# Chunk attention and a bilinear feed-forward layer: DMA transposes issued from ScalarE's queue, loads of units 5 to 9 earlier in SyncE's

## The chip, the cores and the metric

The kernel runs on one core of a Trainium2 chip. The metric is the device time of an execution in microseconds. TensorE (PE) does the matmuls, VectorE (DVE), ScalarE (ACT) and GpSimd (POOL) work element by element, and SyncE (SP) only issues DMAs here. Each engine works through its own instructions in order.

## The reference

```python
batch, n_heads, seq, head_dim = (8, 8, 576, 64)
n_tokens, d_model, d_ff = (4608, 512, 1536)
...
q_c, k_c, v_c = ...                      # (B, H, 9 chunks, 64, 64)
scores = scale * np.matmul(q_c, k_c.transpose(0, 1, 2, 4, 3))
scores = scores - np.max(scores, axis=-1, keepdims=True)
attn = np.exp(scores)
attn = attn / (np.sum(attn, axis=-1, keepdims=True) + 1e-09)
out = np.matmul(attn, v_c)
...
x = attn_out.transpose(0, 2, 1, 3).reshape(B * S, H * D)
a = x @ w_a
b = x @ w_b
return (a * b @ w_out).astype(np.float32)
```

Attention stays within chunks of 64 tokens. Its result, 4608 tokens of 512 values, goes through a layer with two hidden products a and b of 1536 values, multiplied element by element, and an output product back to 512 values. Inputs and result are float32.

## The kernel before

**Tiling.** Tokens are worked in 9 blocks K of 512, and each block in two units of 256 tokens, so that there are 18 units u. A unit is four chunks of 64 tokens with all eight heads. Unit u belongs to block u // 2. Matmuls are in bf16 and accumulate in PSUM.

**A unit's way to its attention.** `load_unit(u)` brings q, k and v of the unit from HBM into three float32 tiles `f32[u % 3][x]`, each in two DMAs of 256 KB (line 123), or in four of 128 KB where the unit crosses from one batch entry to another. `cast_unit(u)` casts them to bf16 on GpSimd (line 171): q and k into `qkb[u % 2]`, v into `vb[u % 3]`. `turn_unit(u)` is one DMA transpose of 512 KB from `qkb[u % 2]` to `qkT[u % 3]` (line 215). Then come, on TensorE, `scores(u)` (line 233, into the PSUM tile PS), on ScalarE `expo(u)` (line 244), and later `sums(u)` (line 250) and `values(u)` (line 266); ScalarE takes a logarithm and an exponential for the reciprocal (lines 276, 280), and `normalise` on VectorE (line 285) writes x transposed, `xT`. Units 0 to 3 are turned on TensorE with helpers of their own; the DMA transpose serves units 4 to 17.

**The layer.** `ffn(K, ft)` is one of 12 steps of a block: four matmuls for b and four for a (line 397), each 128x128 by 128x512, into two of the four PSUM banks of the ring F. `ffn_close` copies b to SBUF on ScalarE (line 408, tile `bsb`), and VectorE multiplies it with a into `ab[ft]` (line 409). In block 1 the first seven steps are done in two halves of 256 tokens. The output product is `outs` in blocks 0 and 1 (lines 419 and 429), and `outs_fast` from block 2 on (lines 466 to 511), which needs fewer products but sums of the weights, `sum_wo(i)` on GpSimd (lines 453 to 456), and of a·b, `sum_ab`. In `outs_fast` ScalarE copies m3 and m4 (lines 495 and 501).

**The order.** It is written out by hand (`tc.manual_schedule`), and the instructions of each engine stand in the order of the program. `slot(uv, us)` puts attention between steps: sums and values of unit uv, then scores of unit us; the exponent and the normalisation that follow wait in the list `late`, and `step()` emits one of them before each step. In the steady part, blocks 2 to 8, `slot` comes after steps 1 and 8, `cast_unit(u + 1)` one step later, `turn_unit(u + 1)` and `load_unit(u + 3)` three steps later. Every load, store and transpose is issued from SyncE, one behind the other. The transitional part is blocks 0 and 1, where the weights have just been loaded and units 4 to 9 are brought in; its order is listed step by step, and it is this part that the change rewrites.

**Synchronisation.** The framework that builds the program adds the waits. A DMA waits for its data and for its buffer; its completion is counted on one of eight counters, and a DMA also waits until the one before it on the same counter has landed.

Of the kernel before, what the change touches and what calls it, by code (L numbers as in the profile page):

```python
# [11 lines left out]
def kernel(  # L12
# [10 lines left out]
    nc = tc.nc  # L23
# [57 lines left out]
    NP = NFT // 2  # L81
# [25 lines left out]
    def nextF():  # L107
        return ring("f", F)
# [9 lines left out]
    def load_natural(u, x, src, eng):  # L118

        t = f32[u % NF32][x]  # L120
        for g in range(2):
            for p, n, b, s0 in runs(u, g):
                eng.dma_start(  # L123
                    out=t[p:p + n, g * 512:(g + 1) * 512].rearrange("p (h d) -> p h d", h=H),
                    in_=src[b, :, s0:s0 + n, :].transpose([1, 0, 2]),
                )
# [47 lines left out]
    def cast_qk(u, x, eng):  # L174
        copy(eng, qkb[u % 2][:, x, :], f32[u % NF32][x])

    def cast_pairs(u, x, eng):
        copy(
            eng,
            qkb[u % 2][:, x, :].rearrange("p (r h d) -> p h r d", r=2, h=H),  # L180
            f32[u % NF32][x].rearrange("p (h r d) -> p h r d", h=H, r=2),
        )

    def cast_v(u, eng, pieces=1):
        n = 1024 // pieces
        for i in range(pieces):
            copy(eng, vb[u % 3][:, n * i:n * i + n], f32[u % NF32][2][:, n * i:n * i + n])
# [26 lines left out]
    def transpose_dma(u, eng):  # L214
        eng.dma_start_transpose(
            out=qkT[u % 3], in_=qkb[u % 2].rearrange("p x c -> p (x c)")
        )

    def scores(u, pairs=False):
        t = qkT[u % 3]  # L220
        tp = t[:, 0:8, :].rearrange("p (r m) t -> p m r t", r=2)
        for g in range(2):
            for m in range(4):
                c = g * 256 + m * 64
                for j in range(2):
                    for cl in range(2):
                        o = PS[cl * 64:cl * 64 + 64, j, c:c + 64]
                        qt = t[j * 64:j * 64 + 64, 4 * g + m, cl * 64:cl * 64 + 64]
                        if pairs:
                            n = (2 * g + cl) * 32  # L230
                            o = o.rearrange("p (t r) -> p r t", r=2)
                            qt = tp[j * 64:j * 64 + 64, m, :, n:n + 32]
                        nc.tensor.matmul(  # L233
                            o,
                            t[j * 64:j * 64 + 64, 8 + 4 * g + m, cl * 64:cl * 64 + 64],
                            qt,
                            start=True,
                            stop=True,
                        )
# [6 lines left out]
    def sums(u, SU, c0=0, c1=512):  # L246
        e = E[u % 2]
        for j in range(2):
            for cl in range(2):
                nc.tensor.matmul(  # L250
                    SU[cl][j * 64:j * 64 + 64, c0:c1],
                    ones[cl * 64:cl * 64 + 64, :],
                    e[cl * 64:cl * 64 + 64, j, c0:c1],
                    start=True,
                    stop=True,
                )

    def values(u):
        e = E[u % 2]
        for g in range(2):  # L260
            for m in range(4):
                c = g * 256 + m * 64
                for cl in range(2):
                    for j in range(2):
                        h = 2 * m + j
                        nc.tensor.matmul(  # L266
                            PA[j * 64:j * 64 + 64, cl, c:c + 64],
                            vb[u % 3][cl * 64:cl * 64 + 64, g * 512 + h * 64:g * 512 + h * 64 + 64],
                            e[cl * 64:cl * 64 + 64, j, c:c + 64],
                            start=True,  # L270
                            stop=True,
                        )

    def log_sums(u, SU):
        for cl in range(2):
            nc.scalar.activation(out=lns[:, cl, :], in_=SU[cl], func=AF.Ln)  # L276

    def inverse(u, cl=None):
        s = slice(0, 2) if cl is None else slice(cl, cl + 1)
        nc.scalar.activation(out=inv[u % 2][:, s, :], in_=lns[:, s, :], func=AF.Exp, scale=-1.0)  # L280
# [132 lines left out]
    def ffn(K, ft, us=(0, 1)):  # L413
        banks = nextF(), nextF()
        ffn_products(K, ft, us, range(NKT), banks)
        ffn_close(K, ft, us, banks)
# [20 lines left out]
    def outs(K, tgs):  # L437
        o = [nextF() for _ in tgs]
        for ft in range(NFT):
            for k, tg in enumerate(tgs):  # L440
                out_products(tg, ft, o[k])
        for k, tg in enumerate(tgs):
            out_close(K, tg, o[k])
# [5 lines left out]
    def sum_wo(i, eng):  # L449

        b = staged["o", i].rearrange("p (x c) -> p x c", x=4)
        y = wsum[:, i]
        eng.tensor_tensor(out=y[:, 0:2], in0=b[:, 0:4:2], in1=b[:, 1:4:2], op=ADD)  # L453
        eng.tensor_tensor(out=y[:, 2], in0=b[:, 1], in1=b[:, 3], op=SUB)  # L454
        eng.tensor_tensor(out=y[:, 3], in0=b[:, 2], in1=b[:, 0], op=SUB)  # L455
        eng.tensor_tensor(out=y[:, 4], in0=b[:, 0], in1=b[:, 3], op=ADD)
# [64 lines left out]
    with tc.manual_schedule():  # L521
# [10 lines left out]
        V, A, G = nc.vector, nc.scalar, nc.gpsimd  # L532
# [100 lines left out]
        def load_unit(u, xs=(0, 1, 2)):  # L633
            if u < NU:
                for x in xs:
                    load_natural(u, x, (q, k, v)[x], nc.sync)

        def cast_unit(u, xs=(0, 1, 2)):
            if u < NU:
                for x in xs:  # L640
                    if x < 2:
                        cast_qk(u, x, G)
                    else:
                        cast_v(u, G)

        def turn_unit(u):
            if u < NU:
                transpose_dma(u, nc.sync)

        def turn_pairs(u, x, engs):  # L650
            evacuate_pairs(u, x, transpose_pairs(u, x), engs)
# [3 lines left out]
        def drain():  # L655
            while late:
                fn, a = late.pop(0)
                fn(*a)

        def slot(uv, us, pairs=False, short=False):  # L660


            drain()
            if uv is not None:
                SU = nextF(), nextF()
                sums(uv, SU)
                values(uv)
                log_sums(uv, SU)
                if short:
                    for cl in range(2):  # L670
                        late.extend([(inverse, (uv, cl)), (normalise, (uv, cl))])
                else:
                    inverse(uv)
                    late.extend([(normalise, (uv, 0)), (normalise, (uv, 1))])
            if us is not None:
                scores(us, pairs)
                late.append((expo, (us,)))

        def step():
            if late:  # L680
                fn, a = late.pop(0)
                fn(*a)
# [26 lines left out]
        cast_pairs(3, 1, G)  # L709
        cast_unit(3, (2,))  # L710
        cast_pairs(2, 1, V)
        load_unit(5, (0,))
        o = nextF(), nextF()
        for ft in range(NFT):
            for tg in range(2):
# [23 lines left out]
        slot(None, 3, True)  # L739
        drain()  # L740
        cast_unit(4)
        turn_unit(4)
        load_unit(5, (1, 2))
        load_unit(6)
        cast_unit(5)

        for ft in range(7):
            step()
            ffn(1, ft, (0,))
            if ft == 1:  # L750
                slot(3, None, short=True)
            if ft == 3:
                turn_unit(5)
                load_unit(7)
        for ft in range(7):
            step()
            ffn(1, ft, (1,))
            if ft == 3:
                slot(None, 4)
                cast_unit(6)  # L760
        for ft in range(7, NFT):
            step()
            ffn(1, ft)
            if ft == 8:
                turn_unit(6)
                load_unit(8)
                sum_wo(1, G)
            if ft == 10:
                slot(4, 5)
                sum_wo(2, G)  # L770
                cast_unit(7)
        for tg in range(4):
            step()
            outs(1, (tg,))
            if tg == 1:
                slot(5, 6)
                turn_unit(7)
                load_unit(9)
                for i in range(3, NP):
                    sum_wo(i, G)  # L780
        for K in range(2, NBLK):
            for s in range(NFT + 2):
                step()
# [44 lines left out]
```

## Time and profile before

| | |
|---|---|
| time, median of 13 runs | 328.43 us (326.3 to 331.25) |
| the profiled execution: time, span | 328.94 us, 327.2 us |
| PE busy | 309.3 us (95%) |
| DVE, ACT, POOL busy | 185.8 (57%), 133.1 (41%), 124.9 (38%) us |
| DMA moved | 55.00 MB, mean 168 GB/s |
| DMA transposes (line 215) | 14, issued by SyncE, 5.0 us from issue to landing (median) |
| loads of 256 KB (line 123) | 28 each of q, k and v, 4.2 to 4.4 us to landing (median) |

The span is the time between the first and the last instruction that the profile shows; the profiled execution's own time is 1.7 us longer. A busy share is an average over the whole span: what a wait costs is to be read from the stage in which it stands. In the profile's timelines SPq is SyncE's queue of DMA issues; an issue's length is not the time until its data have landed. The text in square brackets at the end of a line is the idle time of the engine just before it, and what ended it.

### The profile page before, as it was taken

What the parts mean: (1) busy time and instruction counts of PE and PEld (TensorE: products, weight loads), DVE (VectorE), ACT (ScalarE), POOL (GpSimd) and SP (SyncE); (2) the same over time, 40 slices, a digit from 0 to 9 for tenths busy, and PEclk for the clock granted to TensorE, in tenths of its full rate; (3) what the DMA queues carried; (4) which work ended last, traced back from release to release, by engine and by line L of the source; (5) the groups of instructions that cost most, each with busy time, mean ns of one, the idle gap of its engine ahead of it and who ended that gap; (6) DMA issues with size and microseconds to landing.
All of it is one profiled execution on the core that took longest, in us unless ns stands there. A gap on an engine that the chain in (4) does not pass through costs nothing.

```text
span 327.2 us, 7303 instructions
## 1 busy us (share of the span) xinstructions
PE 309.3 (95%) x2910; PEld 178.6 (55%) x2910; DVE 185.8 (57%) x369; ACT 133.1 (41%) x224; POOL 124.9 (38%) x161
## 2 busy tenths in 40 slices
PE   6689989996995999999999999999999999999994
PEld 3444445863442448644854485458445844684473
DVE  2344434533245666596568747875787467646662
ACT  3343315644143452356244614461546163513320
POOL 2758857326995302810280039003900400050022
PEclk9569999999898999999999999999999999999999
DMA  7999998989979999899159918991510110011003
GB/s 224 258 352 387 394 281 198 272 202 243 220 171 217 206 231 198 254 225 238 57 144 215 233 44 125 252 230 64 154 42 0 67 66 0 2 65 66 0 1 128
DMA packets 145698, 55.00 MB, mean 168 GB/s; under 512 B 126208, under 2 KB 139520, under 8 KB 145664
## 3 DMA queue, kind: packets, MB, share of 16 engines
q1 hardware_dynamic: 145664, 54.54, 66.1%
q8 instruction: 22, 0.36, 0.4%
q14 instruction: 12, 0.10, 0.1%
HBM read 37.75 MB, written 9.44 MB: 144 GB/s over the span
## 4 chain that ended last, share of the span: by engine, by line
PE 81%; POOL 5%; DMA 5%; SPq 4%; issue 2%; DVE 2%; POOLq 0%; ACT 0%; DVEq 0%
PE F L397 53%; PE F L475 19%; PE F L419 3%; SPq L123 3%; DMA f<-in_k_dram 2%; DMA qkT<-qkb 2%; POOL wst L453 2%; PE PS L233 1%; PE F L250 1%; DMA f<-in_v_dram 1%; PE PA L266 1%; POOL wst L454 1%; DVE qkT L171 1%; POOL qkb L171 1%; POOL wst L455 1%
## 5 line engine op out<-in xcount | busy, mean ns | idle before, releaser
L397 PE MATMUL F<-xT,wb 128*128 128x512 bf16 (+1 forms) x460 | 115.5, 373 | 0.9 <-DVE xT L383 0.9
L397 PE MATMUL F<-xT,wa 128*128 128x512 bf16 (+1 forms) x460 | 114.7, 371 | 0.0
L408 ACT CAST bsb<-F 128x512 bf16<-128x512 f32 (+1 forms) x115 | 64.1, 559 | 112.6 <-PE F L397 111.2
L409 DVE TENSOR_TENSOR ab<-F,bsb 128x512 bf16<-128x512 f32 (+1 forms) x115 | 75.3, 656 | 60.9 <-PE F L397 54.3
L397 PEld LDWEIGHTS <-wa 128*128 128x128 bf16 x460 | 45.3, 99 | 49.9 <-issue 2.9
L397 PEld LDWEIGHTS <-wb 128*128 128x128 bf16 x460 | 44.2, 99 | 46.9 <-issue 3.8
L493 POOL TENSOR_TENSOR part<-part 128x256 f32<-128x256 f32 x14 | 10.1, 724 | 143.7 <-ACT part L501 143.7
L171 POOL CAST qkb<-f 128x1024 bf16<-128x1024 f32 (+1 forms) x37 | 35.6, 976 | 23.7 <-DMA f<-in_q_dram 12.1
L475 PEld LDWEIGHTS <-wst 128*128 128x128 bf16 x420 | 41.1, 98 | 4.7
L475 PE MATMUL F<-wst 128*128 128x256 bf16 x252 | 33.6, 273 | 0.0
L285 DVE TENSOR_TENSOR xT<-PA,inv 128x512 bf16<-128x512 f32 x32 | 21.8, 683 | 15.2 <-ACT inv L280 15.2
L493 DVE TENSOR_TENSOR osb<-F,part 128x256 f32<-128x256 f32 x56 | 22.3, 419 | 10.7 <-POOL part L493 10.7
L171 POOL CAST vb<-f 128x1024 bf16<-128x1024 f32 (+2 forms) x22 | 20.2, 919 | 11.7 <-DMA f<-in_v_dram 10.4
L493 POOL TENSOR_TENSOR part<-part,osb 128x256 f32<-128x256 f32 x28 | 19.7, 724 | 12.2 <-DVE osb L493 12.2
L276 ACT ACTIVATE lns<-F 128x512 f32<-128x512 f32 x32 | 17.4, 594 | 14.5 <-PE F L250 14.5
L419 PE MATMUL F<-wo,ab 128*128 128x512 bf16 x96 | 22.1, 379 | 0.9 <-DVE osb L429 0.9
L475 PE MATMUL F<-wst,ab 128*128 128x256 bf16 x168 | 22.9, 273 | 0.0
L244 ACT ACTIVATE E<-PS 128x1024 bf16<-128x1024 f32 (+1 forms) x20 | 18.8, 941 | 8.6 <-PE PS L339 5.6
L463 DVE TENSOR_TENSOR wst<-ab 128x512 bf16<-128x512 bf16 x42 | 20.9, 498 | 0.0
L464 DVE TENSOR_TENSOR wst<-ab 128x512 bf16<-128x512 bf16 x42 | 20.9, 497 | 0.0
L475 PE MATMUL F<-wo,wst 128*128 128x256 bf16 x168 | 20.6, 273 | 0.0
L493 DVE TENSOR_TENSOR part<-F,part 128x256 f32<-128x256 f32 x14 | 6.0, 425 | 22.7 <-POOL part L493 22.7
(49 smaller groups left out, 197.6 us busy)
## 6 DMA issues: line engine op xcount, KB each, us to landing
out_dram<-osb SPq DMA_DIRECT2D x32, 256.0 KB, 2.6
f<-in_q_dram SPq DMA_DIRECT2D x28, 256.0 KB, 4.2
f<-in_k_dram SPq DMA_DIRECT2D x28, 256.0 KB, 4.4
f<-in_v_dram SPq DMA_DIRECT2D x28, 256.0 KB, 4.4
wst<-in_moe_w_out_dram SPq DMA_DIRECT2D x6, 512.0 KB, 9.1
wst<-in_moe_w_b_dram SPq DMA_DIRECT2D x5, 512.0 KB, 7.6
wst<-in_moe_w_a_dram SPq DMA_DIRECT2D x5, 512.0 KB, 7.8
f<-in_v_dram SPq DMA_DIRECT2D x16, 128.0 KB, 3.2
```

The costliest lines, as they stand in the source:

```text
L171: eng.tensor_copy(out=out, in_=in_)
L244: nc.scalar.activation(out=e[:, :, s], in_=PS[:, :, s], func=AF.Exp, scale=scale)
L276: nc.scalar.activation(out=lns[:, cl, :], in_=SU[cl], func=AF.Ln)
L285: nc.vector.tensor_tensor(out=x.rearrange("p m (g c t) -> p c g m t", g=2, c=2)[:, cl], in0=PA[:, cl, :].rearrange(shape, g=2, m=4), in1=i ...
L397: nc.tensor.matmul(bank[:, 0:n], w[ft // 2][ft % 2][:, kt, :], x[:, kt, us[0] * 256:us[0] * 256 + n], start=(kt == 0), stop=(kt == NKT - 1),)
L408: nc.scalar.copy(out=bT[:, 0:n], in_=banks[0][:, 0:n])
L409: nc.vector.tensor_tensor(out=ab[ft][:, us[0] * 256:us[0] * 256 + n], in0=banks[1][:, 0:n], in1=bT[:, 0:n], op=MULT)
L419: nc.tensor.matmul(o, ab[ft][:, tg * 128:(tg + 1) * 128], wo[ft // 2][:, ft % 2, :], start=(ft == 0), stop=(ft == NFT - 1),)
L463: nc.vector.tensor_tensor(out=y[:, 0:2], in0=a[:, 0:2], in1=a[:, 2:4], op=ADD)
L464: nc.vector.tensor_tensor(out=y[:, 2:4], in0=a[:, 1:3], in1=a[:, 0:4:3], op=SUB)
L475: nc.tensor.matmul(o, a(i)[:, c:c + 128], b(i), start=(i == 0), stop=(i == NP - 1))
L493: eng.tensor_tensor(out=out, in0=in0, in1=in1, op=op)
```

## The change

`turn_unit` issues its transpose from ScalarE's queue, and SyncE keeps loads and stores alone. In the steady part the places of the calls stay the same; there, too, each transpose now stands between ScalarE's evacuations. In the transitional part the calls move. All of load 5 comes ahead of the output product of block 0. The transposes of units 4 to 7 have new places among the steps. Loads 7, 8 and 9 are called at earlier steps, cast 6 before the second half of the steps, cast 7 after step 8. `slot(4, 5)` moves from step 10 to step 8, and the five calls of `sum_wo` are spread anew.

```diff
         def turn_unit(u):
             if u < NU:
-                transpose_dma(u, nc.sync)
+                transpose_dma(u, nc.scalar)
...
         cast_pairs(2, 1, V)
-        load_unit(5, (0,))
+        load_unit(5)
         o = nextF(), nextF()
...
         cast_unit(4)
-        turn_unit(4)
-        load_unit(5, (1, 2))
         load_unit(6)
         cast_unit(5)
 
         for ft in range(7):
             step()
             ffn(1, ft, (0,))
             if ft == 1:
                 slot(3, None, short=True)
-            if ft == 3:
-                turn_unit(5)
+            if ft == 5:
+                turn_unit(4)
                 load_unit(7)
+        cast_unit(6)
         for ft in range(7):
             step()
             ffn(1, ft, (1,))
             if ft == 3:
                 slot(None, 4)
-                cast_unit(6)
+            if ft == 4:
+                turn_unit(5)
+                load_unit(8)
+        sum_wo(1, G)
         for ft in range(7, NFT):
             step()
             ffn(1, ft)
             if ft == 8:
+                slot(4, 5)
+                cast_unit(7)
+            if ft == 9:
                 turn_unit(6)
-                load_unit(8)
-                sum_wo(1, G)
-            if ft == 10:
-                slot(4, 5)
+                load_unit(9)
                 sum_wo(2, G)
-                cast_unit(7)
+                sum_wo(3, G)
         for tg in range(4):
             step()
             outs(1, (tg,))
             if tg == 1:
                 slot(5, 6)
+                sum_wo(4, G)
+                sum_wo(5, G)
+            if tg == 2:
                 turn_unit(7)
-                load_unit(9)
-                for i in range(3, NP):
-                    sum_wo(i, G)
         for K in range(2, NBLK):
```

## The prediction

> **What bounds the kernel now.** I read the busy slices first, then the waits of TensorE, then the timelines of TensorE, SyncE, GpSimd and ScalarE about the two places where TensorE stands still. In the slices each digit is a fortieth of the span, 8.18 us.
>
> ```profile
> PE   6689989996995999999999999999999999999994
> ACT  3343315644143452356244614461546163513320
> PEclk9569999999898999999999999999999999999999
> DMA  7999998989979999899159918991510110011003
> ```
>
> TensorE is full from the fourteenth slice (106 us) to the last, so nothing can be won there by moving transfers. Before that it dips in slice 10 (73.6 to 81.8 us, 6) and slice 13 (98 to 106 us, 5); the clock dips with or just after each. The start (slices 1 to 3) is not touched by the change. The DMA engines are near full as long as units are loaded ahead. TensorE's waits between 42 and 120 us:
>
> ```profile
> PE PS L233 <- DMA qkT<-qkb: 6.4, 2, 3.5
> PE F L419 <- DVE osb L429: 0.9, 1, 0.9
> ```
>
> So both dips are the scores (L233) waiting for a DMA transpose. TensorE's timeline gives the waits and what the lowered clock costs after them (start, length, count, idle before):
>
> ```profile
> 80.96 0.64 PE L233 MATMUL PS<-qkT 64*64 64x64 bf16 x32 [2.86 <-DMA qkT<-qkb]
> 81.53 1.89 PE L397 MATMUL F<-xT,wb 128*128 128x512 bf16 x4
> 83.22 1.46 PE L397 MATMUL F<-xT,wa 128*128 128x512 bf16 x4
> 84.51 5.34 PE L419 MATMUL F<-wo,ab 128*128 128x512 bf16 x24
> ...
> 103.87 0.44 PE L233 MATMUL PS<-qkT 64*64 64x64 bf16 x32 [3.51 <-DMA qkT<-qkb]
> 104.25 1.63 PE L397 MATMUL F<-xT,wb 128*128 128x512 bf16 x4
> 105.68 1.91 PE L397 MATMUL F<-xT,wa 128*128 128x512 bf16 x4
> 107.38 1.32 PE L397 MATMUL F<-xT,wb 128*128 128x512 bf16 x4
> 108.54 1.03 PE L397 MATMUL F<-xT,wa 128*128 128x512 bf16 x4
> ```
>
> A step of eight such matmuls takes 1.73 us elsewhere (starts 70.41 and 72.13). After the first wait it takes 84.51 - 81.53 = 2.98 (1.25 lost), after the second 107.38 - 104.25 = 3.13 and 109.40 - 107.38 = 2.02 (1.7 lost together). The two waits with their aftermath cost 2.86 + 1.25 + 3.51 + 1.7 = **9.3 us**. That is all this change can take from TensorE.
>
> Why are those transposes late? SyncE's queue and GpSimd's casts:
>
> ```profile
> 73.79 1.98 SPq L123 DMA_DIRECT2D f<-in_v_dram  x2
> 75.89 2.94 SPq L215 DMA_TRANSPOSE qkT<-qkb  x1
> ...
> 94.66 2.67 SPq L123 DMA_DIRECT2D f<-in_v_dram  x4
> 97.43 1.05 SPq L435 DMA_DIRECT2D out_dram<-osb  x2
> 98.58 3.19 SPq L215 DMA_TRANSPOSE qkT<-qkb  x1
> ...
> 136.31 1.32 SPq L215 DMA_TRANSPOSE qkT<-qkb  x1
> ```
>
> The transpose of unit 5 is issued at 75.89, but its last cast started at 68.88 and ended at 69.92: SyncE was issuing the six loads of unit 6 from 67.77 on. That of unit 7 is issued at 98.58, with its cast done at 88.75 (two casts from 86.73, 2.02 together): SyncE was at the twelve loads of unit 8 and two stores. They stood 6.0 and 9.8 us in a queue behind transfers that they don't need. They land 5.0 and 5.2 us after issue.
>
> **What the Trainium skill says.** "Perfetto Trace Analysis", section "DMA Instruction — HWDGE": the shown length of such an issue is the wait for the descriptor generator, which is locked for one user, plus the generation, and not the data movement. The trace agrees: an issue takes 1.32 to 4.11 us here, and the data land 3.6 to 6.9 us after its start. "DMA: Bandwidth & Descriptors", section "Issuing engines are not separate DMA queues": DMAs of several issuers run on the same 16 engines, and a second issuer saves only issue time. No run shows two issuers yet. "TensorE: Matmul & The Clock Gate", section "Part 1: The HAM clock gate": after an idle window of about 3.4 us the clock is halved until it has been busy as long again. The trace agrees roughly: after 2.86 and 3.51 us of waiting the granted clock averages 0.72 in the 6 us that follow.
>
> **The change part by part.** *Removed:* 14 transposes from SyncE, median 2.69 us each there; SyncE isn't the bound after 106 us, so only the two late ones pay. *Added:* the same 14 on ScalarE, which does nothing else meanwhile. Their length D there isn't in the trace. Lower bound 1.3 us (136.31, nothing queued ahead), upper bound 4.1 (the longest of before, at 111.14, behind loads). I take **D = 2.0**: ScalarE's queue has no loads of its own ahead, so 1.3, plus about 0.7 for the load that SyncE is just generating (0.6 to 1.0 us each).
>
> What queues behind a transpose on ScalarE is the evacuation of TensorE's b banks (L408), then VectorE's product (L409), then the bank's next use. F has four banks, a step takes two, so a bank comes round two steps later.
>
> ```profile
> 62.65 0.37 ACT L408 CAST bsb<-F 128x256 bf16<-128x256 f32 x1 [0.52 <-PE F L397]
> 63.58 0.37 ACT L408 CAST bsb<-F 128x256 bf16<-128x256 f32 x1 [0.56 <-PE F L397]
> ...
> 68.83 0.84 ACT L408 CAST bsb<-F 128x256 bf16<-128x256 f32 x2
> ```
>
> - Unit 4, after step 5 of the first half: issue from 63.06; the next copy ends at 63.06 + D + 0.04 + 0.37 and its product 0.46 later. TensorE needs them at 64.69 and 65.12. Slack 1.15: stall D - 1.15 = 0.85.
> - Unit 5, after step 4 of the second half: the exponential has just kept ScalarE, the copy ends at 69.25; the next ends at 69.27 + D + 0.41, and TensorE wants that bank at 70.41. Stall D - 0.7 = 1.3.
> - Unit 6, after step 9 with 512 columns: copies are 0.59, a step 1.73. Copy of b at 0 to 0.59, issue at 0.64; the next copy would end at 0.64 + D + 0.63, and the bank is wanted 1.73 + 0.86 + 1.73 = 4.3 after b's end. Slack 3.0: no stall. It also waits for the cast of k of unit 6 (76.83 to 77.87 before); the step's copy ends about 78.3 after the shift of 2.15 - so no wait, or at most some 1.6 us, which the slack mostly covers.
> - Unit 7, after the exponents of slot (5,6): about 88.5, its cast done by 86; free of TensorE's ring. It lands by 94; the scores want it at about 97.
> - Units 8 to 17, at steps 4 and 11: slack 3.0 at step 4. At step 11 the copy of m3 (L495) follows, about 0.9 us later than D = 1.3 allows without a shift; the F bank is asked for again at 3.5 after b's end, so up to D = 2.4 costs nothing. Cost 0 for D = 2.
>
> Do the two stalls go? Unit 5: issue at 69.27 + 0.85 = 70.1, landing at 75.1; the scores, moved from step 10 to step 8, come at about 73.86 + 0.6 + 2.15 = 76.6. Yes, by 1.5 us. Unit 7: yes, by 3.
>
> *Loads.* They don't come as early as the words say: the program gives its DMAs eight completion counters in turn, and a DMA waits for the last one on its counter. The fourth store of block 0 shares a counter with unit 4's transpose, so SyncE holds load 6 until that lands (about 67.5). Load 6 then starts at about 68.2 (67.77 before): no gain. Loads 7 and 8 follow without transposes between, some 4 and 7 us earlier; hidden, as the casts of units 7 and 8 stand behind others on GpSimd. k and v of unit 5 come 5 us earlier, needed so that its transpose can go at 70. The stores of block 0 come some 4 us later; the osb buffers are wanted again only at 87. *Order on GpSimd:* sum_wo(1) to (5), 3.3 us each, move behind casts 6 and 7; the last ends at about 99.6 and cast 8's k at 101.7, its transpose is due at 103.3, the sums are first read past 110. Cost nothing; if GpSimd were 2 us later, ScalarE would wait for cast 8.
>
> Sum: -9.3 + 0.85 + 1.3 = **-7.15 us**, in general -9.3 + (2D - 1.85) up to D = 3. The profiled execution took 328.94 (span 327.2), 0.16% over the median of 328.43; from the median I forecast **321.3**.
>
> **The rivals.**
> 1. *ScalarE becomes the brake (slower).* If the generator serves SyncE's loads first or stands blocked on their full queue, D is 3.6 or more. For: the before shows 3.19 and 4.11 in the loading stretch. Against: there the transposes stood behind loads in the same queue; without that, 1.3 to 1.8. At D = 4: stalls 2.85 + 3.3, about 1.4 at unit 6, and some 1.0 in each of six later loads' steps: 12.6, less 9.3, gives +3.3 us; 331.7. It decides from D = 3.6, where later stalls (D - 3.0, six times) and 2D - 1.85 eat 9.3.
> 2. *One wait stays.* The DMA engines are full to 125 us: a transpose that shares them with loads may land 7 instead of 5 us after issue (6.9 is the longest of before), or load 6 is pushed back by the transpose and ScalarE waits for its cast. Then some 2 us stay at each, clock loss included about 4: gain 3.1, 325.3.
> 3. *Nothing changes.* The counters tie the queues so that the transposes go no earlier; 328. Against: unit 7's needs only its cast and counters of landed transfers.
>
> **How the numbers follow.** Forecast 0.60 (own range D = 1.3 to 2.9: 319.9 to 323.1, with half a per cent of scatter 318.5 to 324.5), rival 2 0.15, rival 3 0.06, rival 1 0.19. A measurement of this kernel can tell about 0.5%, 1.6 us, from no change. Faster 0.60 + most of rival 2 = 0.71; same 0.11; slower 0.18. The range takes in the forecast, rivals 2 and 3 and the mild end of rival 1: 318.5 to 329.
>
> **What would show it.** Right: the wait of L233 for qkT gone or under 1 us, slices 10 and 13 full, transposes on ScalarE of 1.3 to 2.9 us, new TensorE waits of about 1 us on bsb at 65 and 71 us. Wrong: transposes over 3.6 us, ScalarE waiting for GpSimd's casts by microseconds, or TensorE idle at steps 4 or 11 of later blocks.

## The result, and the profile after

The changed kernel takes **333.05 us** (median of 11 runs, 329.6 to 336.78), against 328.11 us for the kernel before in the runs beside it: ratio **1.0121** [1.0089, 1.0152]. (Here and below a ratio counts only those executions of a kernel that lie within 1.5% of its fastest one, while a median counts all of them.) It is 1.2% slower, where 321.3 us was forecast. The profiled execution took 333.93 us, its span 332.1 (327.2 before).

The busy slices of after, each 8.3 us, a digit for each tenth:

```profile
PE   7699989798997799999899999999999999999994
POOL 3658858405699112720273028102800310050022
PEclk9569999979999599999999999999999999999998
DMA  7999999989977643997999936984120410011003
```

TensorE has a small dip in slice 8 (58 to 66 us), another in slice 10, and a large one in slices 13 and 14 (100 to 116 us). In that last dip TensorE waits for no DMA. GpSimd has just been full (699 in slices 11 to 13), and the granted clock falls to 5 in slice 14. TensorE's waits, the parts that are new (in us: total, times, longest):

```profile
PE F L397 <- ACT bsb L408: 5.2, 4, 2.1
PE F L397 <- DVE ab L409: 4.0, 1, 4.0
...
PE F L475 <- ACT part L495: 0.9, 1, 0.9
```

The line for qkT, 6.4 us before, is gone: in this execution no transpose is late. In its place TensorE waits for evacuations. Its timeline says where (start, length, count, idle before):

```profile
66.48 0.60 PE L397 MATMUL F<-xT,wb 128*128 128x256 bf16 x4 [2.12 <-ACT bsb L408]
...
67.48 1.06 PE L397 MATMUL F<-xT,wb 128*128 128x256 bf16 x4
...
70.89 0.45 PE L233 MATMUL PS<-qkT 64*64 64x64 bf16 x32
...
75.89 1.02 PE L397 MATMUL F<-xT,wb 128*128 128x512 bf16 x4 [1.83 <-ACT bsb L408]
...
109.93 1.87 PE L397 MATMUL F<-xT,wa 128*128 128x512 bf16 x4 [4.01 <-DVE ab L409]
...
115.00 1.05 PE L397 MATMUL F<-xT,wb 128*128 128x512 bf16 x4
...
149.69 1.02 PE L397 MATMUL F<-xT,wb 128*128 128x512 bf16 x4 [0.84 <-ACT bsb L408]
```

Later there are two more, 0.88 on `part` at 163.00 and 0.44 on `bsb` at 215.47. Two causes stand behind these waits, and each can be seen on another engine.

**The first is ScalarE**, held by its own DMA issues:

```profile
62.23 3.73 ACTq L215 DMA_TRANSPOSE qkT<-qkb  x1
66.06 0.65 ACT L408 CAST bsb<-F 128x256 bf16<-128x256 f32 x2 [3.52 <-issue]
...
71.97 3.40 ACTq L215 DMA_TRANSPOSE qkT<-qkb  x1
...
75.47 0.65 ACT L408 CAST bsb<-F 128x256 bf16<-128x256 f32 x2 [2.79 <-issue]
```

"<-issue" is time in which the engine waits for nothing that the profile shows; here the issue of the transpose fills it. The transpose of unit 4 begins at 62.23 and holds the next copy of b until 66.06, and the matmul that wants that bank starts at 66.48. So it goes with unit 5. The hold was reckoned at 2.0 us; these are 3.73 and 3.40. All fourteen (ns, minimum/median/maximum):

```profile
L215 ACTq DMA_TRANSPOSE qkT<-qkb x14: 1332/2282/4300, 62.2 to 256.5; - x14
...
DMA to landing us min/median/max: 3.6/6.1/9.3
```

Seven of the fourteen take 2.9 to 4.3 us, six of them while SyncE issues loads or stores, the seventh (2.92 at 92.53) just after SyncE's last load issue had ended at 92.31. Two of the long ones, 4.30 and 3.78, are at 144.65 and 158.75, just ahead of the late waits at 149.69 and 163.00.

**The second is VectorE**, at a step that the prediction did not consider. Its timeline about the 4.01 us wait, and GpSimd's:

```profile
101.41 6.60 DVE L462 TENSOR_TENSOR wst<-ab 128x256 bf16<-128x256 bf16 x1
...
109.20 0.68 DVE L409 TENSOR_TENSOR ab<-F,bsb 128x512 bf16<-128x512 f32 x1
```

```profile
106.83 1.04 POOL L171 CAST qkb<-f 128x1024 bf16<-128x1024 f32 x1
115.10 1.04 POOL L171 CAST qkb<-f 128x1024 bf16<-128x1024 f32 x1 [7.23 <-DMA f<-in_k_dram]
```

A sum of ab (line 462, both operands in SBUF) lasts 6.60 us; elsewhere the same shape takes 0.29. The product (line 409) that TensorE waits for stands behind it. GpSimd works without a gap from 90.78 to 107.87, and the sum ends at 108.01, 0.14 us after GpSimd stops. The product just ahead of the sum, at 100.63, has one input in PSUM and takes its usual 0.69 us beside the same full GpSimd. In the kernel before the same first sum took 2.04 us and ended at 102.68, where GpSimd had run dry at 102.53:

```profile
100.64 2.04 DVE L462 TENSOR_TENSOR wst<-ab 128x256 bf16<-128x256 bf16 x1
```

```profile
101.49 1.04 POOL L171 CAST vb<-f 128x1024 bf16<-128x1024 f32 x1
106.99 1.04 POOL L171 CAST qkb<-f 128x1024 bf16<-128x1024 f32 x1 [4.46 <-DMA f<-in_q_dram]
```

GpSimd's row ends 5.3 us later than before, and its timeline shows where that comes from. It reaches `sum_wo(1)` 1.3 us later (81.49, 80.20 before). Cast 7 now stands ahead of `sum_wo(2)`, and GpSimd idles there for k and v of load 7 (2.15 and 0.80 us). And q of unit 9, which now comes early enough, follows on cast 8 without a gap (1.0).

**The account.** The step after unit 4's hold loses clock: six half groups (four matmuls of 256 columns each) from 66.48 to 70.89 take 4.41 us, where 0.435 each makes 2.61, so 1.80 more. After the blocked sum three groups of 512 columns take 115.00 - 109.93 = 5.07, where 0.865 each makes 2.60, so 2.47 more.

| | us |
|---|---|
| both waits for qkT gone, with their clock (the prediction's own sum) | -9.3 |
| unit 4's hold, and the clock after it | +2.12 + 1.80 |
| unit 5's hold | +1.83 |
| the blocked sum, and the clock after it | +4.01 + 2.47 |
| units 10, 11 and 14 | +0.84 + 0.88 + 0.44 |
| sum | +5.1 |
| spans, 332.1 - 327.2 | +4.9 |

The account closes to 0.2 us in these two executions. Whether its causes hold, and in other executions too, is for the experiments.

### The profile page after: what moved, and what is told of

It is laid out like the page before. It is cut to its first block, busy times and chain, and to the rows that moved or that the text cites. A ratio compares the mean times of both kernels' runs of the same rounds, so it can differ in the third digit from the quotient of the medians.

```text
span 332.1 us, 7332 instructions
## 1 busy us (share of the span) xinstructions
PE 311.4 (94%) x2910; PEld 178.9 (54%) x2910; DVE 188.9 (57%) x369; ACT 132.4 (40%) x224; POOL 125.0 (38%) x161
## 4 chain that ended last, share of the span: by engine, by line
PE 57%; ACTq 3%; POOL 2%; DMA 1%; DVE 1%; issue 1%; ACT 1%; SPq 0%; POOLq 0%; DVEq 0%
PE F L397 37%; PE F L475 17%; ACTq L215 3%; DMA f<-in_v_dram 1%; PE F L250 1%; PE PA L266 1%; PE PS L233 1%; POOL vb L171 1%; POOL part L493 1%; POOL qkb L171 1%; DVE osb L493 0%; ACT bsb L408 0%; SPq L123 0%; POOLq L825 0%; DVE ab L409 0%
## 5 line engine op out<-in xcount | busy, mean ns | idle before, releaser
L397 PE MATMUL F<-xT,wa 128*128 128x512 bf16 (+1 forms) x460 | 116.0, 375 | 4.0 <-DVE ab L409 4.0
L493 DVE TENSOR_TENSOR osb<-F,part 128x256 f32<-128x256 f32 x56 | 22.3, 420 | 10.7 <-POOL part L493 10.7
L462 DVE TENSOR_TENSOR wst<-ab 128x256 bf16<-128x256 bf16 x42 | 19.5, 465 | 1.7
```

Of the source, the lines that this page charges most:

```text
L397: nc.tensor.matmul(bank[:, 0:n], w[ft // 2][ft % 2][:, kt, :], x[:, kt, us[0] * 256:us[0] * 256 + n], start=(kt == 0), stop=(kt == NKT - 1),)
L462: nc.vector.tensor_tensor(out=y[:, 4], in0=a[:, 0], in1=a[:, 3], op=ADD)
L493: eng.tensor_tensor(out=out, in0=in0, in1=in1, op=op)
```

## The experiments

Ratios are to the kernel before, run beside the experiment. My theory after the result: ScalarE's holds at units 4 and 5 (a hold is the time for which an issue keeps ScalarE from its next copy) and the blocked sum eat the gain. Rivals: the moved calls do the harm and not the queue; the blocked sum is chance; or the gain is to be had without ScalarE.

### 1. The queue alone (queue_alone)

The kernel before with this single line changed, all calls at their old places:

```diff
-                transpose_dma(u, nc.sync)
+                transpose_dma(u, nc.scalar)
```

> The kernel before with one edit: the 14 transposes are issued from ScalarE's queue, at the old places. Theory (a transpose holds ScalarE 3.3 to 4.3 us while loads are being generated, and b's evacuation and so TensorE wait behind it): at the old places unit 4 comes ahead of the first step of block 1 and unit 5 after step 3, before its k is cast, so ScalarE is held by the cast as well; TensorE waits on bsb or ab for 2 to 3 us at unit 4 and 5 or more at unit 5, and the wait of 3.5 us for unit 7 may go: 332 to 338 us. Rival (the queue is harmless, it is the new order that loses): 328 us or less, no TensorE wait behind L408 over 1 us.

Measured: 335.51 us, ratio 1.0236 [1.0183, 1.0289]. TensorE's waits, its timeline, and ScalarE's:

```profile
PE F L397 <- ACT bsb L408: 9.2, 3, 7.6
PE F L250 <- ACT bsb L408: 3.0, 1, 3.0
```

```profile
59.65 0.86 PE L250 MATMUL F<-E,ones 64*64 64x512 bf16 x4 [3.02 <-ACT bsb L408]
...
73.53 1.01 PE L397 MATMUL F<-xT,wb 128*128 128x256 bf16 x4 [7.57 <-ACT bsb L408]
```

```profile
63.64 0.37 ACT L408 CAST bsb<-F 128x256 bf16<-128x256 f32 x1 [1.16 <-PE F L397]
69.13 3.41 ACTq L215 DMA_TRANSPOSE qkT<-qkb  x1
72.59 0.63 ACT L280 ACTIVATE inv<-lns 128x512 f32<-128x512 f32 x1 [8.58 <-issue]
```

ScalarE comes to the transpose of unit 5 at 64.01 and stands there until 69.13, because GpSimd's cast of unit 5 (68.06, 1.04 us) is not done; then the issue takes 3.41. All of 8.58 us is shown as "issue". So the new queue is what hurts, and a transpose that is called before its cast is done hurts most. All in all, with the blocked sum that they bring, the moved calls of the full change repair about half of that: 1.0236 becomes 1.0121.

### 2. No loads beside the transposes (no_loads)

```diff
-            if u < NU:
+            if u < 6:
                 for x in xs:
                     load_natural(u, x, (q, k, v)[x], nc.sync)
```

> The changed kernel without the loads of units 6 to 17 (their casts read what lies in the buffers). One look, for the length of a transpose on ScalarE. Theory (it is long only while SyncE's loads are being generated or are in flight): the transposes of units 4 and 5, which took 3.73 and 3.40 us, come to 1.3 to 2, all 14 to under 2.3, and TensorE's waits behind them at 66 and 75 us fall from 2.1 and 1.8 to under 0.8 each. The stores of block 0 still stand at unit 4, so that one may stay longer. Rival (the length belongs to ScalarE's queue or to the stage): units 4 to 7 stay at 2.9 to 3.7.

Measured: 322.09 us (one run). Line 215:

```profile
L215 ACTq DMA_TRANSPOSE qkT<-qkb x14: 1332/1632/4106, 62.1 to 244.4; - x14
...
DMA to landing us min/median/max: 3.6/3.7/6.9
```

The one hold over 2.7 us is unit 4's (4.11), which still has the stores of block 0 and load 5 beside it. Units 5 to 7 take 2.47, 1.63 and 2.62; from unit 8 on all are 1.33 to 1.64, and from unit 10 on they land in 3.6 to 3.8. So most of the length of ScalarE's issue, and most of the late landing, goes with the traffic that SyncE issues. Not all of it: SyncE issued nothing while units 5 and 7 were issued, and 2.47 and 2.62 are above the 2.3 that I had expected. Nor can this run tell whether the issuing of the loads counts or their data under way. TensorE's wait on `bsb` at unit 4 stays (2.48 us, 2.12 in after); that at unit 5 falls from 1.83 to 0.91. The lower bound of D in the prediction was the price without traffic, and it was taken, with a small addition, for a stretch full of traffic.

### 3. Units 4 and 5 back on SyncE (sp45)

After, with two of the fourteen transposes returned to SyncE, ahead of load 6:

```diff
-                transpose_dma(u, nc.scalar)
+                transpose_dma(u, nc.sync if u < 6 else nc.scalar)
...
         cast_unit(4)
-        load_unit(6)
+        turn_unit(4)
         cast_unit(5)
+        turn_unit(5)
+        load_unit(6)
```

The two calls among the steps are left out.

> The changed kernel, with the transposes of units 4 and 5 alone back on SyncE, ahead of load 6; units 6 to 17 stay on ScalarE. Theory (the hold of ScalarE at these two costs TensorE 2.1 + 1.8 of waiting and some 1.8 by the clock): both waits behind bsb go, and no wait for qkT takes their place, since unit 5 is issued by 67. 5.7 us less at this place; but TensorE then comes sooner to block 2, while GpSimd's work ends when it did, so the wait for ab grows from 4.0 by as much as is won, up to the whole: 327 to 333 us. Rival (the holds cost nothing that is not waited for anyway): the waits move to L233 for qkT.

Measured: 329.37 us, ratio 0.9985 [0.9945, 1.0024]. Against after's 1.0121 that is 1.4% or 4.5 us better; by the medians of all executions, 1.003 against after's 1.015, it is 1.2%. The holds of units 4 and 5, with their clock, were 2.12 + 1.80 + 1.83 = 5.75 in the account, and no wait on `bsb` is left. The gain is not theirs alone, as the profiled execution lacks the blocked sum as well (below). And sp45 doesn't beat the kernel before, since waits for qkT come back:

```profile
PE PS L233 <- DMA qkT<-qkb: 6.6, 3, 3.8
```

Two of them count: 3.79 at unit 4, issued only at 64.63 behind k and v of load 5 and stores, and 2.23 at 148.82. Here the first sum took 0.93 us although GpSimd was full:

```profile
99.66 0.93 DVE L462 TENSOR_TENSOR wst<-ab 128x256 bf16<-128x256 bf16 x1
```

```profile
100.39 0.79 POOL L455 TENSOR_TENSOR wst<-wst 128x256 bf16<-128x256 f32 x1
101.14 0.90 POOL L456 TENSOR_TENSOR wst<-wst 128x256 bf16<-128x256 f32 x1
```

Both engines are stretched (GpSimd's two take 0.72 elsewhere) and neither is shut out. So beside a full GpSimd the sum is not always blocked.

### 4. The blocked sum: after again, without the weights' sums, and with the sums moved

`after_again` is after unchanged.

> The changed kernel once more, for a second look. The theory that GpSimd keeps the first sum of ab out (6.60 us on VectorE at 101 us) says that it happens wherever GpSimd works without a gap: over 3 us again, with a TensorE wait for ab of 2 us or more. If it is chance whether the sum gets in between two GpSimd operations (in sp45 it took 0.93 us beside a GpSimd as full), it is about 1 us here, the wait is gone, and this execution is some 6 us shorter than the 332.1 of the first. The holds at units 4 and 5 are as before in either case: 1.5 to 2.7 us of waiting each, transposes of 2.9 to 4.1 us.

Measured: 335.98 us (one run). VectorE, GpSimd and TensorE:

```profile
104.87 6.78 DVE L462 TENSOR_TENSOR wst<-ab 128x256 bf16<-128x256 bf16 x1
```

```profile
110.48 1.03 POOL L171 CAST qkb<-f 128x1024 bf16<-128x1024 f32 x1
```

```profile
113.58 1.86 PE L397 MATMUL F<-xT,wa 128*128 128x512 bf16 x4 [4.25 <-DVE ab L409]
```

The block is there again: 6.78 us, ended at 111.65, where GpSimd's row ends at 111.51. The waits on `bsb` are there again too (2.01 and 1.43), and a third kind, at unit 4, whose transpose landed 11.7 us after its issue at 60.98:

```profile
72.76 0.64 PE L233 MATMUL PS<-qkT 64*64 64x64 bf16 x32 [3.17 <-DMA qkT<-qkb]
```

So the gain of the change is not safe either: of its two profiled executions one has a new wait for qkT.

`no_wsums` takes GpSimd's row away by leaving out three of the weights' sums:

```diff
     def sum_wo(i, eng):
+        if i > 2:
+            nc.vector.memset(wsum[:, i], 0.0)
+            return
```

> The changed kernel without the sums of the weights of pairs 3 to 5 on GpSimd (zeros are written by VectorE in their place), so that GpSimd stands still between the casts of units 7, 8 and 9. If it is GpSimd's work without a gap that keeps the first sum of ab out (6.60 and 6.78 us in two looks, ending 0.14 us after GpSimd's last operation both times), that sum takes under 1 us at about 101 us here and TensorE doesn't wait for ab. If it is a wait for something else (a transpose on ScalarE, a DMA), it stays over 3 us. The holds at units 4 and 5 stay.

Measured: 328.23 us (one run). VectorE (its lines stand three further down):

```profile
101.39 0.29 DVE L465 TENSOR_TENSOR wst<-ab 128x256 bf16<-128x256 bf16 x1
```

At the same time of the execution (101.4) GpSimd is idle (97.49 to 104.03), the sum takes 0.29 us, and TensorE doesn't wait for `ab` at all. TensorE's waits behind ScalarE's holds stay (1.92, 1.77, 1.60), and so does a wait of 2.74 for qkT at unit 4. With GpSimd's row gone the block is gone: it is GpSimd's work that keeps the sum out. sp45 adds that a full row doesn't always do so.

`sums_later` keeps all work and makes the first two sums of block 2 (of ab 0 and 1) five steps later:

```diff
-                    if s % 2:
+                    if K == 2:
+                        if s in (5, 6, 7, 8, 9, 11):
+                            sum_ab({5: 2, 6: 0, 7: 3, 8: 1, 9: 4, 11: 5}[s])
+                    elif s % 2:
                         sum_ab(s // 2)
```

> The changed kernel with one edit: in block 2 the first two sums of ab (steps 1 and 3) are made after steps 6 and 8. Theory (the first operation of these sums, which took 6.60 us on VectorE, was kept out by GpSimd, which worked without a gap from 90.8 to 107.9 us because the early loads had fed it; the product ab behind it came late, and TensorE lost 4.0 us waiting and some 2.5 us by the clock): the wait of TensorE for ab goes, no sum takes over 1.3 us, and the time falls by 5 to 6.5 us against the changed kernel, to about 327. Rival (VectorE was late for another reason, a semaphore or the transpose of unit 8 on ScalarE at 106.0): the wait of some 4 us stays, 333.

Measured: 330.58 us, ratio 1.0040 [1.0011, 1.0068]. That is 0.8% or 2.7 us under after's ratio. The direction is right and the size is not: the profile of after had 4.01 + 2.47 = 6.5 us there. So the full block can't stand in every execution, or part of it comes back elsewhere. In the profiled execution of sums_later (330.94 us) no sum of ab is blocked and TensorE doesn't wait for `ab`, but it waits 3.37 us for qkT at unit 4, and 1.08 at 151.77:

```profile
65.35 0.60 PE L397 MATMUL F<-xT,wb 128*128 128x256 bf16 x4 [2.48 <-ACT bsb L408]
...
66.25 0.60 PE L397 MATMUL F<-xT,wb 128*128 128x256 bf16 x4
...
71.53 0.62 PE L233 MATMUL PS<-qkT 64*64 64x64 bf16 x32 [3.37 <-DMA qkT<-qkb]
```

Four profiled executions have unit 4's transpose at this place in ScalarE's queue. It landed 7.1 us after its issue in after, and TensorE did not wait; it landed 9.6 (no_wsums), 10.7 (sums_later) and 11.7 us (after_again) after it in the others, and TensorE waited 2.74, 3.37 and 3.17 us. So the first profile of after is the one that lacks this wait.

`sp45_sums` adds the same edit to sp45.

> sp45 (the changed kernel with units 4 and 5 back on SyncE) with the first two sums of ab made after steps 6 and 8. sp45 was at 0.9985 of before. If the block of the sums is common there, 0.985 to 0.99 here; if it is chance and rare, equal to sp45 within half a per cent.

Measured: 328.98 us, ratio 1.0006 [0.9969, 1.0042], equal to sp45 within its interval. In the one profile of sp45 the first sum got through in 0.93 us, so that there was nothing to win by moving it, which agrees.

### 5. Can SyncE do it alone, with a better place in its queue?

The rival to the change as a whole: if a place behind loads is what makes a transpose late, put it ahead of them and leave ScalarE out. In `sp_ahead` (the kernel before) unit 5's transpose stands between q and k of load 6, and unit 7's behind unit 6's, ahead of load 8. For that cast 7 was called early, and it overwrites v of unit 4 before its use, so the attention of unit 4 is computed from other values. The calls at the old places, which go, are left out below.

```diff
+        load_unit(6, (0,))
+        turn_unit(5)
+        load_unit(6, (1, 2))
...
                 turn_unit(6)
-                load_unit(8)
                 sum_wo(1, G)
+                sum_wo(2, G)
+                cast_unit(7)
+                turn_unit(7)
+                load_unit(8)
```

> The kernel before, with all transposes left on SyncE, but two of them moved ahead in its queue: unit 5 between q and k of load 6, unit 7 behind unit 6 and ahead of load 8. Theory (what was to be won is the place in the queue, not the queue; ScalarE is free of it): unit 5 issued at about 72, unit 7 at about 89; both waits of L233 go, 9.3 us less, unless the first sums of ab come under GpSimd's work (which ends at 102.5 while block 2 begins some 9 us earlier) and give up to 5 us back: 319 to 324 us. Rival (the DMA engines are full, a transpose brought forward delays loads and a wait comes back elsewhere): 326 to 328.

Measured: 334.55 us, ratio 1.0199 [1.0139, 1.0259]. `sp_ahead_sums` has the sums of experiment 4 moved as well.

> As sp_ahead, with the first two sums of ab of block 2 made after steps 6 and 8. If GpSimd keeps these sums out, this is 2 to 5 us faster than sp_ahead, 318 to 321 us; if not, the two are equal within 1 us.

Measured: 334.89 us, ratio 1.0206 [1.0158, 1.0254]. TensorE stood 14.34 us (13.70 in sp_ahead_sums) at the values of unit 4 for `vb`: the values had to wait for the cast that I had put ahead of them. The edit was at fault, and the two say nothing of the question. `sp_ahead2` mends it; v of unit 7 is cast at its old place:

```diff
-                cast_unit(7)
+                cast_unit(7, (0, 1))
                 turn_unit(7)
...
                 slot(4, 5)
+                cast_unit(7, (2,))
```

> sp_ahead with the cast of v of unit 7 left at its old place, behind the values of unit 4 (in sp_ahead it stood ahead of them and of the buffer's last reader: TensorE waited 14.3 us for it). All transposes on SyncE, unit 5 between q and k of load 6, unit 7 behind unit 6. Theory (the place in the queue was what could be won, 9.3 us in the profile of before): both waits for qkT go, no transpose lands later than 7.2 us after issue, ScalarE is held nowhere; 319 to 324 us, the upper end where the first sum of ab is kept out by GpSimd. Rival (full DMA engines hand the wait to another unit): 326 to 328, a wait of L233 of 2 us or more at unit 6 or 8.

Measured: 329.81 us, ratio 1.0029 [1.0002, 1.0057]. TensorE, and SyncE's queue:

```profile
90.13 0.55 PE L233 MATMUL PS<-qkT 64*64 64x64 bf16 x32 [4.23 <-DMA qkT<-qkb]
...
118.29 0.64 PE L233 MATMUL PS<-qkT 64*64 64x64 bf16 x32 [3.63 <-DMA qkT<-qkb]
```

```profile
84.97 8.59 SPq L215 DMA_TRANSPOSE qkT<-qkb  x2
...
112.79 3.41 SPq L215 DMA_TRANSPOSE qkT<-qkb  x1
```

The waits at units 5 and 7 are gone, and there are two in their place, at units 6 and 8. Unit 8's transpose is issued at 112.79, behind load 9 and two stores. In this order of the one queue the lateness is only handed on. `sp_ahead2_sums` moves the sums as well:

> sp_ahead2 with the first two sums of ab of block 2 made after steps 6 and 8. Block 2 begins some 9 us earlier than before while GpSimd's sums of the weights end as before, so the block of the first sum should be long in sp_ahead2 (over 3 us) and TensorE should wait for ab: then this one is 2 to 6 us faster, 317 to 321 us. Rival: equal within 1 us.

Measured: 330.73 us, ratio 1.0065 [1.0039, 1.0091], with waits of 1.49 and 6.00 us at the same two units. The gain of 2 to 6 us that I had expected from the sums did not come; in sp_ahead2 the first sum had taken 1.73 us, not over 3, and TensorE had not waited for `ab`.

`mixed7` was to be the least form of the change: unit 5 ahead on SyncE as in `sp_ahead`, unit 7 alone on ScalarE at its old call.

```diff
-                transpose_dma(u, nc.sync)
+                transpose_dma(u, nc.scalar if u == 7 else nc.sync)
```

> The kernel before with two edits: unit 5's transpose between q and k of load 6 on SyncE, and unit 7's alone on ScalarE, at its old call, behind the exponents of slot (5,6), where ScalarE has slack. Theory (a hold of 3 to 4 us costs nothing where no evacuation is due behind it): both waits for qkT go, TensorE waits nowhere on bsb, 319 to 325 us, like sp_ahead2. Rival (a transpose in a queue of its own lands so late, 7 us and more beside loads, that the wait of unit 7 comes back): a wait of L233 of 1 us or more at about 95 to 100 us, 324 to 328.

Measured: 333.65 us, ratio 1.0158 [1.011, 1.0206]. ScalarE's queue, SyncE's, and TensorE:

```profile
90.85 1.44 ACTq L215 DMA_TRANSPOSE qkT<-qkb  x1
```

```profile
94.80 1.61 SPq L215 DMA_TRANSPOSE qkT<-qkb  x1
```

```profile
98.51 0.64 PE L233 MATMUL PS<-qkT 64*64 64x64 bf16 x32 [14.27 <-DMA qkT<-qkb]
```

Unit 6's transpose on SyncE starts only at 94.80, when unit 7's on ScalarE, issued at 90.85, had landed 3.8 us later. I take it that the framework that builds the program had put a wait of the one for the other, in its own order. The long wait that follows fills the run, and it too says nothing on the theory.

### 6. ScalarE only where its evacuations have slack (four_act)

After, with units 6 to 9 on ScalarE and the rest on SyncE. Unit 4 goes ahead of k and v of load 5, unit 5 between q and k of load 6, and block 2's sums are moved as in experiment 4 (the sums and the old calls of units 4 and 5, which go, are left out):

```diff
-                transpose_dma(u, nc.scalar)
+                transpose_dma(u, nc.scalar if 6 <= u < 10 else nc.sync)
...
-        load_unit(5)
+        load_unit(5, (0,))
...
         cast_unit(4)
-        load_unit(6)
+        turn_unit(4)
+        load_unit(5, (1, 2))
         cast_unit(5)
+        load_unit(6, (0,))
+        turn_unit(5)
+        load_unit(6, (1, 2))
```

> What the runs point to, put together: the changed kernel with transposes of units 6 to 9 alone on ScalarE (where its evacuations have slack); unit 4 on SyncE ahead of k and v of load 5, unit 5 on SyncE between q and k of load 6, units 10 to 17 on SyncE as before; the first two sums of ab in block 2 after steps 6 and 8. If the holds at units 4 and 5 and in blocks 3 to 8 and the blocked sums are the whole loss of the changed kernel, and the late transposes of units 5 and 7 the 9.3 us that could be won, then TensorE waits nowhere over 1 us after 60 us: 319 to 323 us, 0.97 to 0.985 of before. Rival (the loads of units 6 to 9 on full DMA engines set the pace up to block 2, and a wait taken away comes back at the next unit, as in sp_ahead2): a wait for qkT of 2 us or more stays, 326 to 329.

Measured: **323.83 us** (6 runs, 323.14 to 324.88), ratio **0.9858** [0.9826, 0.989]. It beats both kernels, though it lies just outside the 319 to 323 us expected. Its waits:

```profile
PE PS L233 <- DMA qkT<-qkb: 2.9, 2, 2.3
...
PE F L397 <- ACT bsb L408: 1.4, 1, 1.4
```

The waits for qkT are 2.26 us at unit 5, still on SyncE, and 0.66 at unit 7. So a wait over 2 us stayed, as the rival said, but the time is far under the rival's 326. ScalarE's issues of units 6 to 9 take 1.43, 3.82, 2.15 and 2.43 us. Unit 7's 3.82 keeps no copy of b waiting, as it stands in the output product; what it costs is the 0.66, as its data landed 9.4 us after the issue. Unit 8's is what is left of the first cause:

```profile
104.70 2.15 ACTq L215 DMA_TRANSPOSE qkT<-qkb  x1
106.95 1.07 ACT L408 CAST bsb<-F 128x512 bf16<-128x512 f32 x2 [4.48 <-POOL qkb L171]
```

ScalarE stood for GpSimd's cast of unit 8 (done at 104.67) and then for the issue, 4.48 us in all, of which 1.42 reached TensorE. SyncE is relieved just in the stretch in which its queue is longest (loads 7 to 10), and the first sum of ab in block 2, at 108.37, comes after GpSimd's row and takes 0.29 us. Which of the edits brings how much of the 1.4% was not taken apart.

## Why the prediction was wrong

- **What bounds the kernel; the gain of 9.3 us: right for units 5 and 7.** Both waits were due to SyncE's queue, and both are gone in after and in after_again. In queue_alone they are gone too (0.93 us is left, at unit 8), but there TensorE had waited over 10 us before.
- **"I take D = 2.0": the term that was mis-sized first.** Measured 3.73, 3.40, 3.32 and 2.92 for units 4 to 7. The text gave 1.3 to 4.1 as bounds and chose near the lower, because ScalarE's queue has no loads of its own ahead. no_loads shows that a queue of its own helps little as long as SyncE's traffic runs beside it. "Perfetto Trace Analysis", section "DMA Instruction — HWDGE", cited in the prediction, had pointed there: the generator is shared, and a wait for its lock is part of the shown length. The traces agree in the main: in after it is 1.33 to 1.65 us with nothing beside, and up to 4.3 beside SyncE's traffic. It is not the whole rule: at 178.91 in after an issue beside loads took 1.33, and at 92.53 one with no SyncE issue beside it took 2.92. What decides there is open.
- **The formulas for units 4 and 5: right in kind, too high in size.** With the true D, D - 1.15 = 2.58 and D - 0.7 = 2.70; measured 2.12 and 1.83. Together the two stalls are 1.8 us more than forecast.
- **Left out: the clock after a new wait.** It was priced for the waits that go and not for those that come; after unit 4's hold in after it cost 1.80. Not every such wait costs it: after 2.48 us at the same place in sums_later there was no loss.
- **"Do the two stalls go?": asked of units 5 and 7 alone.** Unit 4's transpose moved too. With the prediction's own figures it would land at 63.06 + 5.0 = 68.1 and its scores would come at 67.40 + 0.85 = 68.25, so the slack was 0.2 us. Landing 9.6 to 11.7 us after issue it cost 2.74 to 3.37 in three of four profiled executions. The first profile of after has no such wait: the data landed at 69.3, and the scores, late by the hold and the clock, came at 70.89.
- **"Units 8 to 17 ... Cost 0 for D = 2": failed with D.** At 4.30, 3.78 and 3.93 us three of them cost 0.84, 0.88 and 0.44. The slack of 3.0 was about right: unit 10's 4.30 - 3.0 = 1.3 stands against 0.84.
- **"Order on GpSimd: ... Cost nothing": the step that failed outright.** It asked whether the sums and casts come in time for their readers, and they do, though the last sum of the weights ended at 103.93 and not at 99.6. It didn't ask who shares anything with GpSimd while it is busy. The change itself fills GpSimd there: GpSimd comes late to `sum_wo(1)` and stands idle in cast 7, so that the sums and casts that follow run without a gap over the first sum of ab and beyond it. This cost 4.01 + 2.47 us in the first profiled execution of after and 4.25, without the clock after it, in the second; no_wsums removes it. "SBUF — State Buffer", section "Who interferes with whom", has the rule that was needed: a VectorE instruction with both inputs in SBUF contends with a GpSimd instruction that reads SBUF, the shared port is an exclusive lock, and the order of issue decides who blocks. The traces agree that the sum is held, and that the product with one input in PSUM is not (0.69 us at 100.63). They show more than the page says: the sum was held not for one GpSimd instruction but for the whole row of them, until 0.14 us after its end, and in sp45 it got in between.
- **Load 6 and the counters: right in kind.** SyncE issued the last store of block 0 only at 69.46, just after unit 4's transpose had landed at 69.3, as the text had it, and load 6 at 69.89 (68.2 forecast). TensorE has no wait that goes back to it.
- **The rivals.** Rival 1, ScalarE as the brake, came near with its 331.7, but by luck. Its terms, 2.85 + 3.3 + 1.4 and six times 1.0, make 13.6 and not 12.6. And that price was for ScalarE alone, whose waits with their clock make 2.12 + 1.80 + 1.83 + 0.84 + 0.88 + 0.44 = 7.9 in after: without the blocked sum the account ends below zero. Rival 2 was half right: with two issuers a transpose lands later (median 6.1 us, 5.0 before, and 11.7 once). That fits the cited section "Issuing engines are not separate DMA queues", by which DMAs of several issuers share the same 16 engines. The wait came at unit 4, not at the two that the rival named.

What stays open: how often the sum is blocked. Both profiled executions of after show it whole, moving it won only 2.7 of 6.5 us, and sp45 let it through in 0.93. No run put `sum_wo(2)` back ahead of cast 7 with the rest of the change kept, and none tells a generator that is taken from DMA engines that are full.

## What to carry to other kernels

A DMA issue on ScalarE cost that engine its whole issue time here, 1.3 us alone and up to 5.1 beside another queue's traffic: price it under that traffic, call it only when its data are ready, and put it where the evacuations behind it have that much slack. When work is moved so that an engine has no gaps left, look up who shares SBUF with it and what of theirs falls into that stretch, and count the clock after each new wait as a possible cost, as for those removed. A transpose moved forward in a full queue made the next one late here; relief for a short stretch (four of fourteen transposes, with units 4 and 5 ahead in SyncE's queue and the sums moved) was worth more than moving all. And one profile is not enough: of four executions alike at unit 4 the first was the only one without a wait there.

## What the runs showed of the hardware that was not expected

- A sum of ab on VectorE caught beside GpSimd ended when GpSimd paused, in five executions alike. End of the sum and end of GpSimd's row: 102.68 and 102.53 (before), 108.01 and 107.87 (after), 111.65 and 111.51 (after_again), 103.55 and 103.42 (sp_ahead2), 100.07 and 99.93 (no_loads): 0.13 to 0.15 us apart each time, with sums of 1.05 to 6.78 us. In sp45 it got in between instead, at 0.93 us. What decides between the two was not found.
- The granted clock can fall after shorter waits than the kernel before had shown, but the length of the wait doesn't decide it. In after 2.12 us at 66.48 was followed by about half speed (1.06 us where 0.60 is usual) until 70.89, in after_again 2.01 us at 65.14 likewise (mean clock 0.56 to 69). After 1.83 us at 75.89 in after, 2.48 at 65.35 in sums_later and 2.74 at 70.30 in no_wsums it did not fall (mean clock 1.00 in the 4 us that follow). What decides was not found.
- An issue of the same transpose of 512 KB takes 1.33 to 4.30 us in one execution of after (5.06 at most, in no_wsums), and its data land 3.6 to 11.7 us after its start.
